# Eight weight pieces prepared beside the attention of two batches, and the first gate unit between its last steps

## Chip, cores and metric

The kernel runs on one core of a Trainium2 chip. Its time is the device time in microseconds, the median of several runs. Times inside it are from one profiled execution and count from the start of its span.

## What is computed

```
q, k, v: (4 batches, 12 heads, 448 tokens, 64); g_q, g_k: (64)
attn = softmax(rmsnorm(q, g_q) @ rmsnorm(k, g_k)^T / 8) @ v     # per batch and head
x = attn as (1792 tokens, 768)
y = (silu(x @ w_gate) * (x @ w_val)) @ w_out                    # 768 -> 1536 -> 768
h = y @ w2_in                                                   # 768 -> 2048
out = (h * cos(h)) @ w2_out                                     # 2048 -> 768, float32
```

Weights arrive as 64-bit floats. Each is turned into float32 by three VectorE instructions on its integer halves, scaled by a power of two and split into a high and a low 16-bit part; a product is then three matmuls.

## The kernel before

Heads go in pairs: pairs 0 to 5 are batch 0, 6 to 11 batch 1, and so on; a pair has seven steps of 128 rows (two heads of 448).

**Attention of batches 0 and 1.** One loop counts `n`. Step `n` of `c_step` makes the transposed scores of one row block (`c_st`, banks "c"), their exponential on ScalarE, and the product with V (`c_av`, banks "t" and "u"); twelve steps ahead `c_s` makes scores for the row maximum that VectorE takes from the three "s" banks. The row sums of a pair go through DRAM and back (`c_x`, `c_sum`, `c_inv`, `c_out`, `c_back`, `c_mul`, `c_lo`, over eleven steps) before its output `X` can be used; the last pair, 11, does it on the chip (`c_x`, `c_half`). The pair of batch 2 that comes next is prepared beside it.

**Weights.** A piece is three 128-row blocks of 256 columns. `w_load` brings it (768 KB, into one of three "raw" tiles), `w_conv` makes it float32 (VectorE L932 to L934) and sums its squares (ScalarE L952), `w_scale` makes the scale of a unit of two pieces from a small matmul (L959) and four small VectorE instructions, `w_split` makes the parts (ScalarE L964, VectorE L965), and the next `w_store` writes them to scratch (384 KB). Pieces 0 to 11 are gate and value units of columns 0 to 2 in turn (two gate pieces, two value pieces), 12 to 17 the output product of these columns, 18 to 35 the same again. The table `WSTEP` tells at which steps of the attention loop pieces are loaded, converted and split.

**Visits.** After that loop its pools are closed (the "c" and "u" banks become the four "mm" banks), and a visit runs the 18 matmuls of one piece on one batch (`mm_piece`, L1093 to L1095). Two pieces are visited for batch 0, then the same two for batch 1, 72 visits for pieces 0 to 35. Beside them run the 53 steps of the attention of batch 2, spread over the visits by `SCH`. At a piece's first visit `w_loads(j + LA)`, `w_conv(j + CA)`, `w_scale(j + CA - 1)` and `w_split(j + 2)` work ahead (`LA` 5, `CA` 4). `fin_gate` and `fin_val` take the banks out (ScalarE L1131, VectorE L1132, L1140).

**What sets the order.** A scheduler places instructions on each engine by its own timeline. What goes through `InOrder` stays in the order of the code while its engine is named in `in_order`: SP's queue and GpSimd during the attention loop. Through this helper all instructions show the helper's line (L156).

Of the kernel before, what the change touches and what calls it, by code (L numbers as in the profile page):

```python
# [164 lines left out]
def kernel(ctx: ExitStack, tc, q, k, v, g_q, g_k, w_gate, w_val, w_out, w2_in, w2_out, out):  # L165
# [3 lines left out]
    gps = InOrder(tc, nc.gpsimd, "POOL", in_order)  # L169
    B, H, S, D = q.shape  # L170
# [197 lines left out]
    def v_row(b):  # L368
        ps = bank(ps_s, "s")
        tc.keep_in_program_order(nc.tensor.matmul(ps[:1, :P], vmx.pop(b)[:, 2:3], ident, start=True, stop=True))  # L370
# [8 lines left out]
    def v_out(b):  # L379
        ps = bank(ps_s, "s")  # L380
        tc.keep_in_program_order(nc.tensor.matmul(ps[:, :2], full[:1], vmx.pop(b)[:, 2:4], start=True, stop=True))
# [87 lines left out]
    def s_mm(n):  # L469
# [6 lines left out]
        for i in range(2):  # L476
            for h in ((0, 1), (1, 0))[i]:
                hs = slice(HP * h, HP * h + HP)
                nc.tensor.matmul(  # L479
# [79 lines left out]
    def a_r(g):  # L559
        rd = Rs[g]  # L560
        if "rp" in cfg(g):
            ps = bank(ps_s, "s")
            nc.tensor.matmul(ps[:, :S], ones, rd.rearrange("p t q -> p (t q)"), start=True, stop=True)
# [11 lines left out]
    def a_av(g, part):  # L575
# [7 lines left out]
        for n in range(nn * part // 4, nn * (part + 1) // 4):  # L583
# [76 lines left out]
    def c_s(n):  # L660
# [26 lines left out]
    def c_st(n):  # L687
# [6 lines left out]
        for k, (wt, off, mv) in enumerate(((T, NS, T), (C, 0, Bq))):  # L694
            for h in ((0, 1) if h0 is None else (h0,)):
# [4 lines left out]
                nc.tensor.matmul(  # L700
# [4 lines left out]
    def c_av(g, j):  # L705
# [3 lines left out]
        for h in range(2):  # L709
# [3 lines left out]
            nc.tensor.matmul(pg["o"][h][:, :S], colv[g % 2][rows, j, h], e[rows], start=(j == 0), stop=(j == 3))  # L713
# [241 lines left out]
    def unit_scale(u):  # L955
        q = nrm_t.pop(u)
        ps = bank(ps_s, "s")
        for i, n in enumerate(q):
            nc.tensor.matmul(ps[:, :1], full, n[:, 0:1], start=(i == 0), stop=(i == len(q) - 1))  # L959
# [29 lines left out]

    def w_loads(upto):  # L990
# [7 lines left out]
    def w_conv(j):  # L998
        if j >= len(pieces) or not pieces[j]["fresh"] or pieces[j]["kind"] == "out2":
            return  # L1000
# [481 lines left out]
```

## Time and profile before

| | us |
|---|---|
| median of 3 runs | 1308.86 |
| the runs | 1307.93 to 1309.38 |
| the profiled execution, whole | 1306.7 |
| its span | 1304.9 |
| TensorE busy in the span | 1201.7 |
| VectorE busy | 830.6 |
| ScalarE busy | 646.2 |

The times in this document's rows are those of the profiled execution. It lies 2.2 us below the median. A matmul counts as busy to its modelled end, so that neighbours overlap; the pace is the distance of two starts.

### The profile page before, as it was taken

What the parts mean: (1) busy time and instruction counts of PE and PEld (TensorE: products, weight loads), DVE (VectorE), ACT (ScalarE), POOL (GpSimd) and SP (SyncE); (2) the same over time, 40 slices, a digit from 0 to 9 for tenths busy, and PEclk for the clock granted to TensorE, in tenths of its full rate; (3) what the DMA queues carried; (4) which work ended last, traced back from release to release, by engine and by line L of the source; (5) the groups of instructions that cost most, each with busy time, mean ns of one, the idle gap of its engine ahead of it and who ended that gap; (6) DMA issues with size and microseconds to landing.
All of it is one profiled execution on the core that took longest, in us unless ns stands there. A gap on an engine that the chain in (4) does not pass through costs nothing. (4 is left out here: it accounts for less than half of the span.)

```text
span 1304.9 us, 18162 instructions
## 1 busy us (share of the span) xinstructions
PE 1201.7 (92%) x6460; PEld 674.3 (52%) x6460; DVE 830.6 (64%) x1577; ACT 646.2 (50%) x1224; POOL 405.1 (31%) x309
## 2 busy tenths in 40 slices
PE   1898997888999979999999999999999998999998
PEld 0333333343774437744468546855555545666665
DVE  5876766989978896068844698487888885100000
ACT  3566673555555643356662454477776784100000
POOL 7755203344612254034552114413323222000000
PEclk9999998899999999999999999999999998999999
DMA  5544653866988778479768787630121237522121
GB/s 147 134 105 101 174 174 104 202 186 179 263 271 228 207 195 264 171 187 225 161 136 273 238 314 260 228 128 1 49 73 49 107 122 249 176 68 93 59 91 43
DMA packets 223532, 209.96 MB, mean 161 GB/s; under 512 B 147281, under 2 KB 178897, under 8 KB 223441
## 3 DMA queue, kind: packets, MB, share of 16 engines
q1 hardware_dynamic: 223440, 208.80, 55.4%
q8 instruction: 50, 0.82, 0.3%
q14 instruction: 42, 0.34, 0.1%
HBM read 136.87 MB, written 41.57 MB: 137 GB/s over the span
## 5 line engine op out<-in xcount | busy, mean ns | idle before, releaser
L1093 PE MATMUL mm<-xy,wp 128*128 128x448 f16 x840 | 299.9, 358 | 19.9 <-DVE ga L1132 7.0
L1094 PE MATMUL mm<-xy,wp 128*128 128x448 f16 x840 | 299.8, 357 | 0.8 <-POOL xy L156 0.8
L1095 PE MATMUL mm<-xy,wp 128*128 128x448 f16 x840 | 295.7, 356 | 2.2 <-DVE wp L965 2.2
L1106 PEld LDWEIGHTS <-g 128*128 128x128 f16 x1344 | 132.3, 98 | 92.8 <-issue 6.9
L1093 PEld LDWEIGHTS <-wp 128*128 128x128 f16 x960 | 96.5, 100 | 108.6 <-issue 18.7
L1094 PEld LDWEIGHTS <-wp 128*128 128x128 f16 x960 | 95.3, 99 | 95.8 <-issue 17.3
L1095 PEld LDWEIGHTS <-wp 128*128 128x128 f16 x960 | 94.6, 99 | 93.2 <-issue 5.7
L156 POOL TENSOR_TENSOR g<-tmp,g 128x448 f16<-128x448 f32 x64 | 71.0, 1123 | 175.5 <-ACT g L1252 175.5
L1093 PE MATMUL mm<-g,wp 128*128 128x448 f32 x288 | 106.9, 371 | 0.0
L1095 PE MATMUL mm<-g,wp 128*128 128x448 f32 x288 | 105.3, 366 | 0.0
L1094 PE MATMUL mm<-g,wp 128*128 128x448 f32 x288 | 104.7, 364 | 0.0
L1106 PE MATMUL mm<-wp,g 128*128 128x384 f16 x576 | 101.1, 330 | 3.8 <-DVE tmp L1248 3.8
L1106 PE MATMUL s<-wp,g 128*128 128x384 f16 x576 | 100.2, 328 | 0.0
L156 POOL TENSOR_TENSOR g<-ga,g 128x448 fp32r<-128x448 f32 x48 | 66.4, 1396 | 108.2 <-ACT g L1142 107.9
L498 ACT ACTIVATE pr<-s,sm,esc 128x448 f32<-128x448 f32 x84 | 60.2, 719 | 64.8 <-DVE sm L492 55.0
L156 POOL TENSOR_TENSOR wp<-w,wp 128x768 fp32r<-128x768 f32 x36 | 70.2, 1954 | 69.2 <-ACT wp L1033 44.0
L156 POOL TENSOR_TENSOR p<-pr,p 128x448 f16<-128x448 f32 x36 | 44.0, 1226 | 125.5 <-ACT p L522 83.4
L156 POOL TENSOR_TENSOR ri<-ss,half 128x14 f32<-128x14 f32 x24 | 63.9, 2662 | 57.1 <-DVE ss L347 32.2
L488 DVE TENSOR_REDUCE sm<-s 128x1 f32<-128x448 f32 x84 | 51.0, 615 | 45.0 <-PE s L479 44.9
L1264 ACT ACTIVATE tmp<-mm,osc 128x384 f32<-128x384 f32 x8 | 4.6, 580 | 148.6 <-PE mm L1106 147.8
L952 ACT ACTIVATE raw<-w 128x768 f32<-128x768 f32 x56 | 46.9, 838 | 54.6 <-DVE w L934 42.7
L932 DVE TENSOR_SCALAR w<-raw 128x768 int32<-128x768 int32 x68 | 49.7, 735 | 37.3 <-POOL wp L156 15.6
(179 smaller groups left out, 2258.5 us busy)
## 6 DMA issues: line engine op xcount, KB each, us to landing
raw<-in_moe_w_out_dram SPq DMA_DIRECT2D x28, 768.0 KB, 5.6
raw<-in_moe_w_in_dram SPq DMA_DIRECT2D x16, 768.0 KB, 5.8
raw<-in_moe_w_gate_dram SPq DMA_DIRECT2D x12, 768.0 KB, 5.5
raw<-in_moe_w_val_dram SPq DMA_DIRECT2D x12, 768.0 KB, 5.2
wp<-scr_gate SPq DMA_DIRECT2D x24, 384.0 KB, 4.6
w<-scr_out SPq DMA_DIRECT2D x24, 384.0 KB, 4.1
wp<-scr_val SPq DMA_DIRECT2D x24, 384.0 KB, 5.4
wp<-scr_out SPq DMA_DIRECT2D x24, 384.0 KB, 3.0
```

The lines of the kernel that those rows point to most:

```text
L156: r = f(*args, **kw)
L488: nc.vector.tensor_reduce(sm[:, 0, t:t + 1], slot[n][:, :S], axis=AX.X, op=ALU.max)
L498: nc.scalar.activation(e, slot.pop(n)[:, :S], AF.Exp, bias=sm[:, 1, t:t + 1], scale=esc, accum_out=sm[:, 2, t:t + 1],)
L932: nc.vector.tensor_scalar(wi, hi, 3, 0x3FFFFFF8, op0=ALU.logical_shift_left, op1=ALU.bitwise_and)
L952: nc.scalar.activation(sq_dst[0], w32, AF.Square, accum_out=n[:, 0:1])
L1093: nc.tensor.matmul(ps[f][:, :S], wh[:, s], x[:, 0], start=(first and i == 0), stop=False)
L1094: nc.tensor.matmul(ps[f][:, :S], wh[:, s], x[:, 1], start=False, stop=False)
L1095: nc.tensor.matmul(ps[f][:, :S], wl[:, s], x[:, 0], start=False, stop=(last and i == n - 1))
L1106: nc.tensor.matmul(ps[:, :CO], x[:, a, p0:p0 + P], rhs, start=st, stop=sp)
L1264: nc.scalar.activation(osb, ps[:, :CO], AF.Copy, scale=ci)
```

## The change

- `WSTEP` is built by a loop: pieces 0 to 7 are loaded, converted, scaled and split at steps 2 to 68 of the attention loop, a unit of two every 16 steps, and pieces 8 and 9 loaded and converted at steps 67 to 78.
- `mm_piece` can run some of a piece's three blocks. The 36 matmuls of the first gate unit on batch 0 run as six blocks at steps 75 to 80, into two "s" banks. Every matmul goes through `InOrder`, and from step 75 to the fourth visit TensorE keeps the order of the code.
- The first four pieces are visited for batch 0, then for batch 1. The first two visits have no matmuls left.
- For pieces below 12, conversion and split run two pieces further ahead (`ahead`), and loads up to 8; `once` keeps a piece from being prepared twice.
- The attention of batch 2 starts at visit 3, not 1.

Line numbers after the change are 7 to 18 higher; matmuls show the helper's line (L163).

```diff
@@ constants @@
+EARLY = 75
-WSTEP = {48: [("load", 2)], 56: [("conv", 0)], 60: [("conv", 1), ("load", 3)], 63: [("scale", 1)], 64: [("split", 0), ("conv", 2), ("load", 4)],
-         70: [("split", 1), ("conv", 3), ("load", 5)]}
+WL = 8
+WAHEAD = 4
+WSTEP = {}
+for _u in range(WAHEAD):
+    for _d, _w in ((-6, ("load", 0)), (-3, ("load", 1)), (0, ("conv", 0)), (4, ("conv", 1)), (7, ("scale", 1)), (8, ("split", 0)), (12, ("split", 1))):
+        WSTEP.setdefault(8 + 16 * _u + _d, []).append((_w[0], 2 * _u + _w[1]))
+for _n, _w in ((67, ("load", 8)), (70, ("load", 9)), (74, ("conv", 8)), (78, ("conv", 9))):
+    WSTEP.setdefault(_n, []).append(_w)
-SCH = ((1, 0), (0, 0), (1, 1))
+SCH = ((1, 0), (3, 0), (1, 1))
@@ w_loads @@
+            if 3 <= nload[0] < NJ and ("conv", nload[0] - 3) not in done:
+                return
@@ attention loop @@
+        if n == EARLY:
+            in_order.add("PE")
+        i = n - EARLY
+        if 0 <= i < KX:
+            if i == 0:
+                cur[0] = [bank(ps_s, "s") for _ in range(2)]
+            mm_piece(i // 3, cur[0], lambda kt: X[kt], (i % 3,))
         step(n, 0)
         w_store()
         w_step(n)
-    in_order.clear()
+    in_order.difference_update(("SP", "POOL"))
@@ visits @@
+    def ahead(j):
+        far = lambda near, t: near + 2 * (t < 2 * KX)
+        for f, near in ((w_conv, CA), (w_scale, CA - 1), (w_split, 2)):
+            for t in range(j, j + near + 3):
+                if t <= j + far(near, t):
+                    f(t)
-    for j0 in range(0, NJ, 2):
+    for j0, j1 in [(0, 4)] + [(j, j + 2) for j in range(4, NJ, 2)]:
         for b in range(2):
-            visits += [(j0, b), (j0 + 1, b)]
+            visits += [(j, b) for j in range(j0, j1)]
...
-                w_loads(j + LA)
+                w_loads(j + (WL if j + WL < 2 * KX else LA))
...
+            if i >= 2:
+                (first bank and mm_piece, as before)
             run_late(i)
             if new:
-                w_conv(j + CA)
-                w_scale(j + CA - 1)
-                w_split(j + 2)
+                ahead(j)
+            if i == 3:
+                in_order.clear()
```

**VectorE beside pairs 2 and 3.** Reductions of the scores are "sm", the integer halves "raw", the float32 piece "w32". Before:

```order
L670 TENSOR_REDUCE sm_836<-s_944 128x1
L677 TENSOR_SCALAR cw_357<-sm_836 128x7
L670 TENSOR_REDUCE sm_978<-s_979 128x1
L678 SCALAR_TENSOR_TENSOR cw_357<-sm_836,cw_357 128x7
L670 TENSOR_REDUCE sm_978<-s_989 128x1
L742 TENSOR_SCALAR sm_970<-sm_970,vsc_104 128x7
L398 TENSOR_TENSOR rqk_926<-rqk_926,ri_1096 128x448
L743 RECIPROCAL sm_970<-sm_970 128x7
L670 TENSOR_REDUCE sm_978<-s_1004 128x1
```

After the change, at the like place of the next pair but one:

```order
L678 TENSOR_REDUCE sm_860<-s_980 128x1
L940 TENSOR_SCALAR w32_1031<-raw_907 128x768
L685 TENSOR_SCALAR cw_357<-sm_860 128x7
L941 SCALAR_TENSOR_TENSOR w32_1031<-raw_907,w32_1031 128x768
L686 SCALAR_TENSOR_TENSOR cw_357<-sm_860,cw_357 128x7
L772 TENSOR_TENSOR tmp_1010<-co_814,cr_952 64x448
L942 SCALAR_TENSOR_TENSOR w32_1031<-raw_907,w32_1031 128x768
L772 TENSOR_TENSOR tmp_1010<-co_815,cr_952 64x448
```

The three conversion instructions of piece 2 now stand between those of the pair, one at a time.

**TensorE at the end of the attention.** "t" and "u" take the products with V, "c" the transposed scores, "s" the scores and now the gate unit ("wp" its weights, "xy" the output of a pair of batch 0). Before, the last steps and the first gate matmul:

```order
L700 MATMUL c_2103<-cB_1786,cC_415 128x448
L713 MATMUL u_2064<-pr_2076,cV_359 128x448
...
L713 MATMUL t_2063<-pr_2088,cV_359 128x448
L713 MATMUL u_2064<-pr_2104,cV_359 128x448
L713 MATMUL t_2063<-pr_2122,cV_359 128x448
L713 MATMUL u_2064<-pr_2122,cV_359 128x448
...
L1093 MATMUL mm_2188<-xy_831,wp_1816 128x448
```

After the change, from the last rows of scores that are turned ("id16") to the second block of the gate unit:

```order
L163 MATMUL s_2076<-id16_106,cw_419 64x128
...
L163 MATMUL s_2091<-xy_855,wp_866 128x448
...
L163 MATMUL s_2092<-xy_855,wp_866 128x448
...
L163 MATMUL c_2099<-T_1659 128x448
...
L163 MATMUL c_2099<-cB_1746,cC_353 128x448
...
L163 MATMUL s_2091<-xy_1009,wp_866 128x448
```

Six matmuls of the unit now stand ahead of each of six steps; the first "mm" matmul is of the value unit.

**VectorE at the joint.** L726 (now L734) is the reciprocal of the last pair, L419 (now L427) the subtraction of pair 12 that the load of pair 13 waits for, L764 (now L772) the last multiplication of a pair. Before:

```order
L764 TENSOR_TENSOR tmp_2071<-co_1940,cr_2039 64x448
L764 TENSOR_TENSOR tmp_2071<-co_1941,cr_2039 64x448
L742 TENSOR_SCALAR sm_2067<-sm_2067,vsc_104 128x7
L408 TENSOR_TENSOR rqk_1976<-rqk_1976,gk_94 128x448
L743 RECIPROCAL sm_2067<-sm_2067 128x7
L726 RECIPROCAL co_2138<-co_2138 128x448
L419 TENSOR_TENSOR h16_2053<-rqk_1976,h16_2053 128x7x64
L764 TENSOR_TENSOR tmp_2146<-co_2139,co_2138 128x448
```

After the change:

```order
L772 TENSOR_TENSOR tmp_2195<-co_2021,cr_2145 64x448
L772 TENSOR_TENSOR tmp_2195<-co_2022,cr_2145 64x448
...
L427 TENSOR_TENSOR h16_2165<-rqk_2056,h16_2165 128x7x64
...
L734 RECIPROCAL co_2268<-co_2268 128x448
...
L772 TENSOR_TENSOR tmp_2276<-co_2269,co_2268 128x448
L772 TENSOR_TENSOR tmp_2281<-co_2160,cr_2265 64x448
L772 TENSOR_TENSOR tmp_2281<-co_2161,cr_2265 64x448
```

The subtraction moved from behind the reciprocal to a place well ahead of it; the multiplication ahead of it is pair 9's in both.

## Rows read from the trace of the kernel before

**Rows 1.** stretches: PE, PEld, DVE, ACT, POOL busy (count), granted clock, DMA share, GB/s
```profile
57.00:139.00 82.00, 73.83 (x315) 28.42 (x314) 58.36 (x127) 54.75 (x100) 44.41 (x31) 0.98 0.49 119
...
206.00:333.50 127.50, 110.18 (x581) 52.31 (x580) 113.12 (x200) 64.76 (x129) 51.87 (x33) 0.94 0.67 174
333.50:390.00 56.50, 55.66 (x299) 45.32 (x298) 48.38 (x78) 30.81 (x76) 22.87 (x13) 1.00 0.94 272
390.00:505.00 115.00, 102.27 (x561) 51.25 (x562) 104.63 (x186) 61.35 (x122) 42.69 (x29) 0.97 0.81 228
...
214.30:333.50 119.20, 101.93 (x546) 48.38 (x544) 108.54 (x195) 62.46 (x125) 51.87 (x33) 0.94 0.68 177
```

**Rows 2.** waits of TensorE, 206 to 333.5 us: total, times, longest
```profile
PE mm L1093 <- ACT wp L964: 5.7, 4, 3.6
```

**Rows 3.** timeline of TensorE at the joints: start, us, instruction, wait ahead
```profile
192.51 1.02 PE L713 MATMUL t<-pr,cV 128*128 128x448 f32 x2 [1.29 <-ACT pr L703]
...
199.54 0.54 PE L713 MATMUL u<-pr,cV 64*128 64x448 f32 x1
206.05 0.53 PE L1093 MATMUL mm<-xy,wp 128*128 128x448 f16 x1 [5.97 <-ACT co L725]
...
214.05 0.35 PE L1095 MATMUL mm<-xy,wp 128*128 128x448 f16 x1
214.24 0.35 PE L1093 MATMUL mm<-xy,wp 128*128 128x448 f16 x1
...
333.49 0.47 PE L1093 MATMUL mm<-g,wp 128*128 128x448 f32 x1
```

**Rows 4.** groups of VectorE and ScalarE, 0 to 206 us: total, mean ns
```profile
L934 DVE SCALAR_TENSOR_TENSOR w<-raw,w 128x768 int32<-128x768 int32 x5 | 4.7, 947 | 0.0
...
L933 DVE SCALAR_TENSOR_TENSOR w<-raw,w 128x768 int32<-128x768 int32 x5 | 4.7, 938 | 0.0
...
L932 DVE TENSOR_SCALAR w<-raw 128x768 int32<-128x768 int32 x5 | 2.7, 547 | 0.0
...
L965 DVE SCALAR_TENSOR_TENSOR wp<-w,wsc,wp 128x768 f16<-128x768 f32 x2 | 2.1, 1036 | 0.4 <-ACT wp L964 0.4
...
L952 ACT ACTIVATE raw<-w 128x768 f32<-128x768 f32 x5 | 4.2, 840 | 0.0
L964 ACT ACTIVATE wp<-w,wsc 128x768 f16<-128x768 f32 x2 | 1.7, 920 | 0.0
```

**Rows 5.** timeline of TensorE, first product with V of pairs 3 and 7
```profile
85.38 1.02 PE L713 MATMUL t<-pr,cV 128*128 128x448 f32 x2 [1.36 <-ACT pr L703]
...
140.62 1.02 PE L713 MATMUL t<-pr,cV 128*128 128x448 f32 x2
```

**Rows 6.** two-operand VectorE lines: mean in 57 to 139; min, median, max
```profile
L398 DVE TENSOR_TENSOR rqk<-rqk,ri 128x448 f32<-128x448 f32 x7 | 5.6, 805 | 0.2 <-POOL ri L156 0.2
...
L398 DVE TENSOR_TENSOR rqk<-rqk,ri x12: 604/618/1369, 13.9 to 134.1; 128x448 f32<-128x448 f32 x12
...
L934 DVE SCALAR_TENSOR_TENSOR w<-raw,w x11: 941/950/2369, 240.5 to 332.2; 128x768 int32<-128x768 int32 x11
```

**Rows 7.** the burst: busy time of ten us, TensorE's wait behind it
```profile
136.00:146.00 10.00, 10.00 (x40) 3.63 (x39) 9.61 (x16) 7.58 (x14) 0.00 (x0) 1.00 0.83 258
...
154.35 1.86 PE L713 MATMUL t<-pr,cV 128*128 128x448 f32 x2 [1.93 <-ACT pr L703]
```

**Rows 8.** timeline of ScalarE, first and last copy of the last pair
```profile
202.95 0.54 ACT L722 ACTIVATE co<-t 64x448 f32<-64x448 f32 x1 [1.77 <-DVE tmp L764]
...
205.37 0.63 ACT L725 ACTIVATE co<-u,vs 64x448 f32<-64x448 f32 x1
```

**Rows 9.** SP's queue at the load of pair 13, TensorE at pair 10
```profile
SPq L156 <- DVE h L419: 23.6, 4, 11.5
...
208.87 0.35 SPq L156 DMA_DIRECT2D rqk<-in_k_dram  x1
...
222.71 0.54 PE L1093 MATMUL mm<-xy,wp 128*128 128x448 f16 x2 [0.69 <-ACT xy L765]
```

More of the change, by code (lines that the diff above doesn't have):

```diff
@@ L169 @@
     gps = InOrder(tc, nc.gpsimd, "POOL", in_order)
+    pe = InOrder(tc, nc.tensor, "PE", in_order)
     B, H, S, D = q.shape
@@ L380, in v_out @@
         ps = bank(ps_s, "s")
-        tc.keep_in_program_order(nc.tensor.matmul(ps[:, :2], full[:1], vmx.pop(b)[:, 2:4], start=True, stop=True))
+        tc.keep_in_program_order(pe.matmul(ps[:, :2], full[:1], vmx.pop(b)[:, 2:4], start=True, stop=True))
         nc.vector.tensor_copy(vsc[:, 2 * b:2 * b + 2], ps[:, :2])
@@ L562, in a_r @@
             ps = bank(ps_s, "s")
-            nc.tensor.matmul(ps[:, :S], ones, rd.rearrange("p t q -> p (t q)"), start=True, stop=True)
+            pe.matmul(ps[:, :S], ones, rd.rearrange("p t q -> p (t q)"), start=True, stop=True)
             if "rv" in cfg(g):
@@ L712, in c_av @@
             e = col[g, 2 * j + h] if j < 3 else col[g, NS - 1]
-            nc.tensor.matmul(pg["o"][h][:, :S], colv[g % 2][rows, j, h], e[rows], start=(j == 0), stop=(j == 3))
+            pe.matmul(pg["o"][h][:, :S], colv[g % 2][rows, j, h], e[rows], start=(j == 0), stop=(j == 3))
     def c_x(g):
@@ L958, in unit_scale @@
         for i, n in enumerate(q):
-            nc.tensor.matmul(ps[:, :1], full, n[:, 0:1], start=(i == 0), stop=(i == len(q) - 1))
+            pe.matmul(ps[:, :1], full, n[:, 0:1], start=(i == 0), stop=(i == len(q) - 1))
         pow2_scale(ps[:, :1], winv[:, u:u + 1], wsc[:, u:u + 1])
@@ L988, with once @@
     nload = [0]
+    done = set()
+    def once(what, j):
+        new = (what, j) not in done
+        done.add((what, j))
+        return new
     def w_loads(upto):
@@ L998, in w_conv @@
     def w_conv(j):
-        if j >= len(pieces) or not pieces[j]["fresh"] or pieces[j]["kind"] == "out2":
+        if j >= len(pieces) or not pieces[j]["fresh"] or pieces[j]["kind"] == "out2" or not once("conv", j):
             return
@@ L1006, in w_scale @@
     def w_scale(j):
-        if j < len(pieces) and pieces[j]["fresh"] and pieces[j]["last"] and pieces[j]["kind"] in ("gate", "val", "h"):
+        if j < len(pieces) and once("scale", j) and pieces[j]["fresh"] and pieces[j]["last"] and pieces[j]["kind"] in ("gate", "val", "h"):
             unit_scale(unit_of(pieces[j]))
     def w_split(j):
-        if j >= len(pieces) or not (pieces[j]["fresh"] or pieces[j]["kind"] == "out1"):
+        if j >= len(pieces) or not (pieces[j]["fresh"] or pieces[j]["kind"] == "out1") or not once("split", j):
             return
@@ L1082, in pre_step, with mm_piece @@
         return done
-    def mm_piece(j, ps, rhs):
+    def mm_piece(j, ps, rhs, steps=None):
         pc = pieces[j]
@@ L1088, in mm_piece @@
         wh, wl = wp_t[j]
-        for i in range(n):
+        for i in range(n) if steps is None else steps:
             x = rhs(pc["k0"] + i)
@@ L1092, in mm_piece @@
                 s = slice(i * 256 + f * P, i * 256 + (f + 1) * P)
-                nc.tensor.matmul(ps[f][:, :S], wh[:, s], x[:, 0], start=(first and i == 0), stop=False)
-                nc.tensor.matmul(ps[f][:, :S], wh[:, s], x[:, 1], start=False, stop=False)
-                nc.tensor.matmul(ps[f][:, :S], wl[:, s], x[:, 0], start=False, stop=(last and i == n - 1))
+                pe.matmul(ps[f][:, :S], wh[:, s], x[:, 0], start=(first and i == 0), stop=False)
+                pe.matmul(ps[f][:, :S], wh[:, s], x[:, 1], start=False, stop=False)
+                pe.matmul(ps[f][:, :S], wl[:, s], x[:, 0], start=False, stop=(last and i == n - 1))
     def mm_out(j, i, ps):
@@ L1105, in mm_out @@
                 st, sp = first and kk == 0 and a == 0 and rhs is wh, last and kk == n - 1 and a == 1
-                nc.tensor.matmul(ps[:, :CO], x[:, a, p0:p0 + P], rhs, start=st, stop=sp)
+                pe.matmul(ps[:, :CO], x[:, a, p0:p0 + P], rhs, start=st, stop=sp)
     def out2_w(j, kk):
@@ L1167, in y_scale @@
         ps = bank(ps_s, "s")
-        nc.tensor.matmul(ps[:, :1], full, n[:, 0:1], start=True, stop=True)
+        pe.matmul(ps[:, :1], full, n[:, 0:1], start=True, stop=True)
         pow2_scale(ps[:, :1], ysc[:, B + b:B + b + 1], ysc[:, b:b + 1])
```

20 lines of the change are left out of this document (10 added, 10 removed).

## The prediction

> **What bounds the kernel now.** I read the stages first: busy time and granted clock in stretches [rows 1]. Up to 206 us the attention of batches 0 and 1 runs; to 333.5 come 24 visits of gate and value pieces (a visit is the 18 matmuls of one weight piece on one batch); to 390 twelve visits of the first output product; to 505 the same 24 visits again with the second half of the columns. In the first set TensorE was busy 110.2 of 127.5 us at a mean clock of 0.94, VectorE 113.1. The second set lasted 115.0 us with VectorE at 104.6. In both, VectorE carries conversions and splits beside the attention of batch 2, and it is the fuller engine.
>
> Next, who TensorE waits for in the first set: 6.0 us for the last copies of the attention stage [rows 3], then 5.7 for the high halves of weights [rows 2]. The times of the joints are read off the timeline [rows 3]: attention ends at 199.54 + 0.54 = 200.1; the first gate matmul starts at 206.05, after a wait of 5.97; its unit has 36 matmuls, and the 37th starts at 214.24, by then 0.187 us after the one before it, the pace of the upper clock level. The first output matmul starts at 333.49.
>
> What must remain of the 119.2 us from 214.3 on? TensorE was busy for 101.9 of them, and a mean clock of 0.94 means that 12% of the stretch stood at the lower level, where half the time is lost: 0.06 x 119.2 = 7.2. So 94.8 us of work at the upper level [rows 1], 17.2 idle, 7.2 to the clock.
>
> **The change part by part.**
>
> *Conversions and splits moved ahead.* Before 206 us VectorE converts 5 pieces and splits 2 [rows 4]; the order puts 11 and 8 ahead of the first gate step. Six more of each: 6 x (0.547 + 0.938 + 0.947) = 14.6 us and 6 x 1.036 = 6.2 [rows 4], with an estimated 1.8 for the scales of three units (small instructions of some 0.15 us): 22.6 us. ScalarE gets 6 x (0.84 + 0.92) = 10.6 us [rows 4]; it was busy 54.8 of 82 us there [rows 1], so there is room.
>
> They fall on steps 8 to 52. A pair's first product with V is step 2 of its seven; pair 3's (step 23) stands at 85.4 and pair 7's (step 51) at 140.6 [rows 5], so a step takes 2.0 us and the six extra pieces land between about 57 and 143. VectorE was busy for 58.4 of the 82 us from 57 to 139 [rows 1]. 58.4 + 22.6 = 81.0: full, before any stall. Stalls there are: GpSimd is busy 44.4 of those 82 us [rows 1], and the two-operand product at L398 took 0.805 us in the mean against 0.604 at best over the stage [rows 6]. At 0.2 us for each of 18 two-operand instructions that is 3.6 us more: 84.6 of the 86 us.
>
> TensorE is what sets the pace there (73.8 of 82 us busy), so what counts is how often it then waits. The nearest row is the one burst that the kernel already has: about 140 to 152 us three conversions beside the largest-value search filled VectorE to 9.6 of 10 us [rows 7]. TensorE then waited 1.93 us for ScalarE, and the product behind the wait took 1.86 us against 1.02 elsewhere [rows 5, 7], a sign of the lower clock level: some 3.5 us for 10.4 us of extra VectorE work (three conversions of 2.43 and the search). Spread out, each of six pairs gets 3.0 + 0.6, a third of that burst: 6 x 1.2 = 7 us, less about 2 because this burst loses its three conversions. I take **5 us**. Ends: -3.5 (the burst's cost goes, nothing comes), and 6 x 3.5 - 3.5 = 17.5 (every pair pays the burst's price).
>
> SP's queue gets 6 loads and 6 stores of 768 and 384 KB, 7.1 MB, put between the transposes and the round trip of the row sums, and a store waits at the head of the queue for its split. About 82 GB/s over 86 us on top of 119 at a DMA share of 0.49; the chip moved 272 at 0.94 later [rows 1]. Behind those waits stand the round trips, eight steps ahead of need, so I cost them at nothing; if that cover is gone, the price is in the 17.5.
>
> *The first gate unit between the steps of the last two pairs.* TensorE runs there without gaps but for 1.29 us [rows 3], so 36 x 0.187 = 6.7 us are added, less the 1.3 that they cover, plus about 0.7 until ScalarE has emptied the two "s" banks that they need: the attention ends at 206.2 without the 5 us above, 211.2 with it. Then the four copies of the last pair must end before "mm" banks exist: before, ScalarE stood behind a VectorE multiplication until 202.95, and the last of the copies began at 205.37 [rows 8]. Here what hangs on that multiplication (pair 9's) stands ahead of the last four exponentials on ScalarE, so it is done by then (were its round trip late, it would now hold them, and TensorE; that is in the 17.5); four copies of 0.54 to 0.63 make 2.3 us, with the hand-over 2.6: 213.8. That is the point that the kernel before reached at 214.3. The gate unit by itself therefore gains what the 5 us cost, and little more. The two "s" banks stay taken until the gate's activation reads them; one is left for the scores of batch 2, which now start at visit 3.
>
> What could be late next is batch 1: its gate unit needs pair 10. Before, the load of pair 13 stood at the head of SP's queue until 208.87, released by VectorE's L419, and behind it pair 10's round trip; TensorE got pair 10 at 222.71 [rows 9]. The order now puts the subtraction L427 (the old L419) that this load waits for ahead of the last pair's reciprocal, not behind it; and TensorE has 36 value and 24 gate matmuls, some 12 us, to do first. Covered.
>
> *The 22 visits that remain.* They are the 94.8 us. From the order, up to the last value step of this set VectorE now has 8 conversions and 4 splits in place of 11 and 10 (it also takes up later pieces sooner): 3 x 2.43 + 6 x 1.04 = 13.5 us less, of 108.5. The kernel before took 119.2 us with 108.5 of VectorE work, the second set 115.0 with 104.6 [rows 1]: both 10.5 us longer than VectorE's work. So 108.5 - 13.5 = 95.0 for VectorE and 94.8 for TensorE: about **105 us**, a loss of 10. Ends: 4 (TensorE 96% busy) and 16 (the second set's loss: 12.7 idle, 3.5 clock).
>
> *After 333.5.* The loads and the output visits stand as before; TensorE was at 55.7 of 56.5 us there. The last 4071 matmuls and 794 VectorE instructions stand in the same order as before. A shift should be kept.
>
> *Sum.* 213.8 + 104.8 = 318.6 against 333.5: 14.9 us less. The profiled execution was 1306.7, so 1291.8; the median of the runs shown is 1308.86, 2.2 above it, so 1294.0. I say **1293**.
>
> **The rivals.**
>
> *Nothing waits in the attention stage, and the visits run as TensorE alone would* (0 and 4 in place of 5 and 10): 11 us more gain, 1282. For: order spreads the conversions one instruction between two reductions. Against: VectorE's 81 of 82 us.
>
> *The visits stay VectorE's*, because the conversions that come sooner fill what was freed (loss 16), or the stage pays more (11): 6 us less gain for each, 12 for both: 1299 to 1305. For: all that is freed is 13.5 us, and VectorE and TensorE are then level.
>
> *Slower: VectorE becomes the bound of the attention stage.* GpSimd and VectorE hold each other up: in the visits L934 took up to 2.369 us against 0.941 at best [rows 6]. If every L933, L934 and L965 of the six pieces met such a stall (1.43 us), VectorE would need 58.4 + 22.6 + 25.7 = 106.7 us in 86. The stage then grows by 21 us, and by more where VectorE also waits for transfers; from 5 + 14.9 = 20 us on, the change loses. 1310 to 1315. Against: GpSimd is idle for half the stretch, and L398's mean shows 0.2, not 1.4. The Trainium skill, "SBUF — State Buffer", section "Who interferes with whom", has a rule for this: a VectorE instruction with two inputs in SBUF and a GpSimd instruction that reads SBUF exclude each other, and the later one blocks entirely. By that rule, 18 instructions met at a share of 0.54 by 1.43 us of GpSimd work, half of it left, wait 18 x 0.54 x 0.72 = 7.0 us, not 3.6; the estimate would then be some 3 us slower, 1296. L398 at 0.805 agrees in kind, with a smaller number.
>
> **How the numbers follow.** Forecast 0.50 (1287 to 1298), larger gain 0.20 (1280 to 1287), smaller gain 0.20 (1298 to 1307), slower 0.10. 0.2% is 2.6 us, about what a measurement of this kernel can tell from no change; of the smaller gain 0.04 lies within it, of the slower case 0.02. Faster 0.86, the same 0.06, slower 0.08. For 8 in 10 the range leaves out the lower end of the larger gain (0.07), the last us of the smaller (0.03) and the slower case: 1282 to 1305.
>
> **What would show it.** The first "mm" matmul near 214 us after a wait of 2 to 3 us in place of 6; in 57 to 143, VectorE above 9 tenths and TensorE's waits for L678 and L711 (the old L670 and L703) up by some 5 us; the first output matmul near 319; from there on the same lengths. Wrong if the attention stage grew by over 10 us, if the visits from the first "mm" to the first output matmul still take over 111 us, or if the second set (115 us) changes by more than 3.

## The result, and the profile after

The changed kernel takes 1298.46 us (median of 4 runs; the kernel before, beside it, 1308.95): a ratio of 0.9919, 95% interval 0.9899 to 0.9938, 10.5 us less. The forecast was 1293, the range 1282 to 1305. The profiled execution has a span of 1297.1 us against 1304.9, so 7.8 of the gain show in it. The total came out near the forecast by luck: the attention stage came out 12.7 us later than summed and the visits 6.7 us shorter, and these errors went opposite ways.

The stages, first of the kernel before (length, then busy time of TensorE, weight loads, VectorE, ScalarE, GpSimd, granted clock, DMA share, GB/s): from the first product with V to the end of the attention of batches 0 and 1, from the first "mm" matmul to the first output matmul, the twelve output visits, the second set of gate and value visits. In the kernel before the second of these stretches still holds the first gate unit; from the 37th matmul on it was 119.2 us [rows 1].

```profile
43.30:200.07 156.77, 143.36 (x609) 55.97 (x607) 112.22 (x237) 104.12 (x190) 61.32 (x45) 0.98 0.55 143
206.05:333.49 127.44, 110.17 (x580) 52.30 (x579) 113.06 (x200) 64.72 (x129) 51.86 (x33) 0.94 0.67 174
333.49:386.10 52.61, 51.77 (x277) 43.07 (x275) 45.10 (x72) 27.86 (x67) 22.88 (x13) 1.00 0.97 283
386.10:499.68 113.58, 100.85 (x558) 48.49 (x557) 102.61 (x187) 62.38 (x125) 40.46 (x27) 0.97 0.80 224
```

The same view of the changed kernel, with the stretch from 57 to 139 us as its second row:

```profile
43.40:223.85 180.45, 153.79 (x657) 63.08 (x655) 140.25 (x287) 116.24 (x213) 67.23 (x47) 0.93 0.63 170
57.00:139.00 82.00, 69.07 (x281) 27.74 (x282) 67.61 (x139) 55.24 (x102) 39.49 (x26) 0.88 0.54 137
226.34:324.47 98.13, 92.40 (x517) 44.30 (x516) 84.33 (x141) 48.92 (x97) 46.38 (x31) 0.98 0.61 155
324.47:385.44 60.97, 56.21 (x288) 44.26 (x287) 48.55 (x85) 35.01 (x82) 22.25 (x15) 0.97 0.78 220
385.44:489.20 103.76, 99.17 (x558) 48.84 (x557) 93.11 (x173) 58.84 (x120) 38.47 (x26) 0.98 0.83 224
```

The attention stage is 23.7 us longer, the visits 29.3 shorter (21.1 from the same point on), the output visits 8.4 longer, the second set 9.8 shorter. From 57 to 139 us VectorE was busy 67.6 of 82 us, not the 81 of the sum, and TensorE 69.1 at a mean clock of 0.88 where it had 73.8 at 0.98 [rows 1]; fewer steps fit into the same time.

The joints in TensorE's timeline of the changed kernel (start, us, instruction, wait ahead), which answer to [rows 3]:

```profile
132.62 1.01 PE L163 MATMUL s<-id,cw 128*64 128x128 f16 x7 [6.72 <-DVE sm L678]
...
192.43 1.02 PE L163 MATMUL t<-pr,cV 128*128 128x448 f32 x2
...
200.43 0.95 PE L163 MATMUL s<-id,cw 128*64 128x128 f16 x7 [3.98 <-DVE cw L686]
201.32 2.33 PE L163 MATMUL s<-xy,wp 128*128 128x448 f16 x6
...
223.31 0.54 PE L163 MATMUL t<-pr,cV 64*128 64x448 f32 x1
...
226.34 5.25 PE L163 MATMUL mm<-xy,wp 128*128 128x448 f16 x18 [2.49 <-ACT co L733]
...
324.47 3.94 PE L163 MATMUL mm<-g,wp 128*128 128x448 f32 x18
```

The attention ends at 223.31 + 0.54 = 223.9 (before 200.1). The wait for the last copies is 2.49 in place of 5.97. The two largest waits inside the attention, 6.72 and 3.98 us, have no counterpart in the kernel before, where the largest after 57 us was 1.93 [rows 7]. The row at 192.43 is pair 10's first product with V; the gate unit's first block follows within this pair. What VectorE did ahead of the first of the two waits:

```profile
119.61 0.19 DVE L686 SCALAR_TENSOR_TENSOR cw<-sm,cw 128x7 f16<-128x7 f32 x1
125.96 0.56 DVE L940 TENSOR_SCALAR w<-raw 128x768 int32<-128x768 int32 x1 [6.17 <-DMA raw<-in_moe_w_gate_dram]
...
131.96 1.14 DVE L678 TENSOR_REDUCE sm<-s 128x1 f32<-128x448 f32 x2
```

At 119.8 us VectorE's next instruction was the conversion L940 of a piece that had not landed; it stood for 6.17 us. The row maxima L678, on which TensorE's score banks wait, came only at 131.96, behind this and behind 6.0 us of other work that stood between. SP's queue in the same stretch:

```profile
110.36 1.55 SPq L163 DMA_TRANSPOSE T<-h  x1
117.79 0.35 SPq L163 DMA_DIRECT2D rc<-sm  x1
118.24 0.37 SPq L163 DMA_DIRECT2D scr_val<-wp  x1
118.67 0.42 SPq L163 DMA_DIRECT2D raw<-in_moe_w_gate_dram  x1
```

SP had stood from 111.9 to 117.79 before the write of the row sums (rc), waiting for VectorE's reciprocal L751. Behind that write stood a store of a split (scr) and the load, so the piece was issued 7.3 us ahead of its use.

### The profile page after: what moved, and what is told of

The parts are those of the page before. It is cut to its first block, busy times and chain, and to the rows that moved or that the text cites. A ratio compares the mean times of both kernels' runs of the same rounds, so it can differ in the third digit from the quotient of the medians.

```text
span 1297.1 us, 18102 instructions
## 1 busy us (share of the span) xinstructions
PE 1198.0 (92%) x6460; PEld 676.1 (52%) x6460; DVE 831.3 (64%) x1577; ACT 645.6 (50%) x1224; POOL 406.8 (31%) x309
## 5 line engine op out<-in xcount | busy, mean ns | idle before, releaser
L163 PE MATMUL mm<-xy,wp 128*128 128x448 f16 x2484 | 491.0, 354 | 5.8 <-DVE ga L1149 3.2
L163 PEld LDWEIGHTS <-wp 128*128 128x128 f16 x2880 | 277.9, 99 | 278.5 <-issue 34.5
L163 PE MATMUL mm<-g,wp 128*128 128x448 f32 x864 | 185.4, 372 | 1.9 <-DVE ga L1157 1.9
L163 PEld LDWEIGHTS <-g 128*128 128x128 f16 x1344 | 132.0, 98 | 91.9 <-issue 5.7
L163 PEld LDWEIGHTS mm<-g,wp 128*128 128x128 f32 x864 | 162.6, 191 | 20.5 <-issue 4.4
L163 POOL TENSOR_TENSOR g<-tmp,g 128x448 f16<-128x448 f32 x64 | 71.2, 1124 | 174.8 <-ACT g L1269 174.8
L163 POOL TENSOR_TENSOR g<-ga,g 128x448 fp32r<-128x448 f32 x48 | 64.8, 1362 | 146.6 <-ACT g L1159 146.5
L163 PE MATMUL mm<-wp,g 128*128 128x384 f16 x576 | 100.8, 330 | 3.6 <-DVE tmp L1265 3.6
L163 PE MATMUL s<-wp,g 128*128 128x384 f16 x576 | 99.3, 326 | 0.0
L163 PE MATMUL s<-T 128*64 128x448 f16 x336 | 63.2, 396 | 36.1 <-DVE T L665 22.6
L163 POOL TENSOR_TENSOR wp<-w,wp 128x768 fp32r<-128x768 f32 x36 | 72.7, 2024 | 59.7 <-ACT wp L1050 39.2
L163 PEld LDWEIGHTS <-T 128*64 128x64 f16 (+1 forms) x432 | 28.4, 109 | 106.5 <-issue 78.5
L942 DVE SCALAR_TENSOR_TENSOR w<-raw,w 128x768 int32<-128x768 int32 x68 | 77.3, 1137 | 0.6
L940 DVE TENSOR_SCALAR w<-raw 128x768 int32<-128x768 int32 x68 | 46.0, 679 | 49.0 <-POOL wp L163 10.6
L163 POOL TENSOR_TENSOR ri<-ss,half 128x14 f32<-128x14 f32 x24 | 63.9, 2663 | 42.3 <-DVE ss L355 33.5
L941 DVE SCALAR_TENSOR_TENSOR w<-raw,w 128x768 int32<-128x768 int32 x68 | 72.5, 1068 | 0.6
L163 POOL TENSOR_TENSOR p<-pr,p 128x448 f16<-128x448 f32 x36 | 41.1, 1147 | 88.0 <-ACT p L530 70.9
```

The lines of the kernel that those rows point to most:

```text
L163: r = f(*args, **kw)
L940: nc.vector.tensor_scalar(wi, hi, 3, 0x3FFFFFF8, op0=ALU.logical_shift_left, op1=ALU.bitwise_and)
L941: nc.vector.scalar_tensor_tensor(wi, hi, -0x40000000, wi, op0=ALU.bitwise_and, op1=ALU.bitwise_or)
L942: nc.vector.scalar_tensor_tensor(wi, lo, 29, wi, op0=ALU.logical_shift_right, op1=ALU.bitwise_or)
```

## Experiments

Each is the changed kernel with the edit shown; lines of an edit are cut to the part that changes. The attention's end is the start of the last "t" matmul plus its 0.54 us, "pair 10" the start of its first product with V. These times are of one profiled execution each; the ratios are medians, to the kernel before on the same chip.

| | ratio | 95% interval | pair 10 | attention ends | first "mm" | first output matmul |
|---|---|---|---|---|---|---|
| kernel before | 1 | | 180.8 | 200.1 | 206.1 | 333.5 |
| changed kernel | 0.9919 | 0.9899–0.9938 | 192.4 | 223.9 | 226.3 | 324.5 |
| loads earlier | 0.9959 | 0.9943–0.9975 | 195.3 | 231.0 | 233.5 | 332.8 |
| pieces only | 0.9958 | 0.9942–0.9975 | 195.5 | 215.0 | 218.9 | 328.5 |
| gate unit only | 0.9997 | 0.9981–1.0012 | 182.6 | 212.8 | 228.8 | 332.6 |
| loads later | 0.9923 | 0.9902–0.9944 | 194.8 | 224.0 | 226.9 | 325.3 |
| short conversions | 0.9949 | 0.9927–0.9972 | 194.7 | 228.5 | 232.9 | 331.4 |
| no loads | 0.9922 | 0.9897–0.9948 | 196.2 | 226.8 | 229.3 | 329.0 |
| three units | 0.9907 | 0.9878–0.9935 | 190.9 | 221.8 | 224.3 | 324.5 |
| two units | 0.9999 | 0.9983–1.0015 | 192.9 | 223.3 | 227.6 | 333.1 |
| products later | 0.9921 | 0.9897–0.9944 | 194.7 | 223.9 | 226.4 | 325.7 |
| both later | 0.9921 | 0.9897–0.9946 | 195.0 | 223.5 | 226.0 | 325.6 |
| order only | 0.9907 | 0.9882–0.9932 | 190.3 | 223.5 | 226.0 | 324.4 |
| units later | 0.9884 | 0.9853–0.9915 | 183.4 | 213.0 | 215.5 | 321.9 |

**The two parts, each alone.** Pieces only:

```
-EARLY = 75
+EARLY = 10 ** 6
-            if i >= 2:
+            if True:
```

> The changed kernel with the first gate unit back behind the attention (the pieces are still prepared beside it). By the prediction's sum the unit's move saves the wait for the last copies (6.0 against 2.6 us) and the 1.3 us that it covers, less some 0.7: the attention then ends at 216 to 217 in place of 223.9, the first mm matmul comes at about 222 and the time is 1301 to 1303. Rival: the unit between the steps costs TensorE as much as it saves, since the 4.0 us wait at 200 us and the lower clock of its first block (2.33 against 1.30 us) come with it: 1296 to 1299.

Gate unit only:

```
-WL = 8
-WAHEAD = 4
-WSTEP = {}
...
+WL = 5
+WSTEP = {48: [("load", 2)], 56: [("conv", 0)], 60: [("conv", 1), ("load", 3)], 63: [("scale", 1)], 64: [("split", 0), ("conv", 2), ("load", 4)],
+         70: [("split", 1), ("conv", 3), ("load", 5)]}
-SCH = ((1, 0), (3, 0), (1, 1))
+SCH = ((1, 0), (0, 0), (1, 1))
-        far = lambda near, t: near + 2 * (t < 2 * KX)
+        far = lambda near, t: near
```

> The changed kernel with the piece preparation of the kernel before (five conversions and two splits beside the attention), the first gate unit still between the last pair's steps. Theory: the gain comes from the visits, which took 98.1 us from the first mm matmul against 119.2 from the same point before, and that needs the pieces prepared ahead; without them the attention ends near 207, the first mm matmul comes near 210, the visits take 115 to 120 us, and the time is 1304 to 1308. Rival: the gate unit's move and the other order of the first visits bring the gain: 1296 to 1300.

The pieces alone give 0.9958 and cost the attention 215.0 - 200.1 = 14.9 us; the gate unit then adds some 5 us of gain by the ratios (0.9958 to 0.9919, measured on different chips, the intervals just apart). Alone it gives nothing (0.9997), and its attention ended at 212.8, not near the 207 expected. The kernel before, the gate unit only and the pieces only, from pair 10 on:

```profile
180.76 1.02 PE L713 MATMUL t<-pr,cV 128*128 128x448 f32 x2
...
187.69 0.58 PE L682 MATMUL s<-id,cw 128*64 128x128 f16 x7 [0.36 <-DVE cw L678]
```

```profile
182.64 1.02 PE L159 MATMUL t<-pr,cV 128*128 128x448 f32 x2
...
190.23 0.80 PE L159 MATMUL s<-id,cw 128*64 128x128 f16 x7 [3.04 <-DVE cw L682]
...
220.98 1.01 PE L159 MATMUL s<-nm,full 128*128 128x1 f32 x4 [7.41 <-ACT pr L502]
...
228.82 0.93 PE L159 MATMUL mm<-xy,wp 128*128 128x448 f16 x2 [0.65 <-ACT wp L968]
```

```profile
195.47 1.02 PE L163 MATMUL t<-pr,cV 128*128 128x448 f32 x2
...
218.91 12.06 PE L163 MATMUL mm<-xy,wp 128*128 128x448 f16 x54 [3.93 <-ACT co L733]
```

This splits the cost of the two parts. Up to pair 10, ahead of the gate unit's first step, the kernels with the pieces are late (changed kernel 192.4 - 180.8 = 11.7 us, pieces only 14.7), the gate unit alone hardly (1.9). From pair 10 to the end the kernel before took 19.3 us and the pieces only 19.5, but the gate unit only 30.1 and the changed kernel 31.4. So the gate unit costs the attention 10.8 to 12.1 us. A part is the wait for "cw" (3.04 and 3.98 us): with TensorE in the order of the code these seven matmuls stand ahead of the unit's first block, where in the kernel before they came after the pair's third product and waited 0.36. That is not all of it: five kernels without a large wait there (loads later, two units, products later, both later, units later) still take 28.4 to 30.4 us.

After the attention of the gate unit only there is no prepared piece left to work on: the first value matmul comes at 228.82, 16 us later. Part of that may be this kernel's own: batch 2's attention starts at the first visit again, and the matmul for the scale of the value pieces waits 7.41 us for ScalarE's L502, which reads batch 2's scores out of a score bank, while the gate unit holds two of the three. In the pieces only, the unit's 36 matmuls run behind the attention, and the 37th comes at about 227.4 (an estimate: 54 matmuls from 218.91, the last 18 at 0.187 us), 1.1 us after the changed kernel's first value matmul. So at the joint the unit's move gains about 1 us; the rest of its gain comes in the visits (first output matmul 4.0 us earlier), and why was not tried.

**Late loads?** The loads of pieces 2 to 9 six steps earlier, and in another kernel three steps later:

```
-    for _d, _w in ((-6, ("load", 0)), (-3, ("load", 1)), (0, ("conv", 0)),
+    for _d, _w in (((-12, -6)[_u == 0], ("load", 0)), ((-9, -3)[_u == 0], ("load", 1)), (0, ("conv", 0)),
-for _n, _w in ((67, ("load", 8)), (70, ("load", 9)),
+for _n, _w in ((60, ("load", 8)), (63, ("load", 9)),
```

> The changed kernel with the loads of weight pieces 2 to 9 issued six steps earlier (seven for pieces 8 and 9); conversions, splits and the gate unit stay where they are. Theory 1, late loads: the attention stage grew because VectorE, which works in order, stands 12.4 us at L940 for pieces that are issued only some 7 us ahead, 6.17 us of it at one piece (TensorE then waits 6.7 us for the row maxima L678 queued behind) and about 3 us ahead of the 3.98 us wait for cw at 200 us. Then the first mm matmul comes at 215 to 218 us in place of 226.3 and the time is 1288 to 1292. Theory 2, VectorE is full: the six extra conversions and splits fill it, whoever it waits for; the waits move to the next row maximum, the first mm matmul stays within 2 us of 226 and the time within 1296 to 1300. Theory 3, VectorE held up by GpSimd: as theory 2, 1296 to 1300.

```
-    for _d, _w in ((-6, ("load", 0)), (-3, ("load", 1)), (0, ("conv", 0)),
+    for _d, _w in (((-3, -6)[_u == 0], ("load", 0)), ((0, -3)[_u == 0], ("load", 1)), (0, ("conv", 0)),
-for _n, _w in ((67, ("load", 8)), (70, ("load", 9)),
+for _n, _w in ((70, ("load", 8)), (73, ("load", 9)),
```

> The changed kernel with the loads of pieces 2 to 9 issued three steps (some 6 us) later, nothing else. Late loads (theory 1): VectorE stands up to 6 us more at each of the eight pieces, and TensorE behind it; with at least half of them reaching TensorE the attention stage grows by 15 to 40 us and the time is 1313 to 1338. VectorE full or held up by GpSimd (theories 2 and 3): the loads are hidden, 1296 to 1301.

Theory 1 fell both ways: earlier loads made the kernel slower by the ratio, later ones changed nothing. (With the loads earlier theories 2 and 3 missed too: first "mm" at 233.5, not within 2 us of 226.) The 6.7 us wait was gone in both, but others came. With the loads earlier, in TensorE's timeline:

```profile
163.92 1.01 PE L163 MATMUL s<-id,cw 128*64 128x128 f16 x7 [5.26 <-DVE sm L678]
```

With the loads later TensorE waited 3.46 us for L678 at 177.7.

**How much work, or how many bytes?** Conversions cut to one of three instructions, and the loads left out:

```
+        if short:
+            return w32
-        w32_t[j] = conv64(raw_t.pop(j))
+        w32_t[j] = conv64(raw_t.pop(j), 2 <= j < 8)
```

> The changed kernel with the conversions of pieces 2 to 7 cut from three VectorE instructions to the first (L941 and L942 left out: 12 instructions of 0.95 us, 11.4 us less VectorE work beside the attention; its weights are therefore wrong). Loads, splits, stores and the gate unit stay. Theory F, the amount of VectorE work fills the engine, and whatever comes late beside it reaches TensorE: the attention ends 7 to 12 us earlier (212 to 217 us in place of 223.9) and the time is 1287 to 1292. Theory L, what costs is the loads and stores in SP's queue and the landing of the pieces: the attention ends at 221 to 226 and the time is 1296 to 1300.

```
+            if 2 <= j < 8:
+                raw_t[j] = raw_t[1, 0]
+                return
...
```

(The rest of the edit keeps piece 1's raw tile in place for this.)

> The changed kernel without the loads of pieces 2 to 7 (4.6 MB beside the attention left out; their conversions read the raw tile of piece 1 again, so its weights are wrong; one mask differs), with the same number of conversions, splits and stores. Theory L: VectorE no longer waits 9 us for pieces 2 to 7, the attention ends at 212 to 217 us and the time is 1287 to 1292. Theory F: VectorE is as full as before, the attention ends at 220 to 226 and the time is 1295 to 1300.

Neither theory held: with 11.4 us of VectorE instructions left out (its busy time fell from 140.3 to 132.9) the attention ended at 228.5, without the loads at 226.8. From the first product with V to the end, with the short conversions:

```profile
42.80:228.46 185.66, 154.98 (x657) 62.50 (x655) 132.87 (x282) 116.07 (x213) 69.15 (x48) 0.95 0.61 167
```

The same without the loads:

```profile
43.40:226.77 183.37, 159.25 (x657) 63.33 (x655) 141.40 (x289) 117.10 (x213) 69.10 (x47) 0.92 0.54 143
```

TensorE stood idle for 185.7 - 155.0 = 30.7 and 183.4 - 159.3 = 24.1 us, against 26.7 in the changed kernel and 13.4 before. So neither half of the added VectorE work nor the loads alone set the end.

**How many units?**

```
-WAHEAD = 4
+WAHEAD = 3
-for _n, _w in ((67, ("load", 8)), (70, ("load", 9)), (74, ("conv", 8)), (78, ("conv", 9))):
+for _n, _w in ((67, ("load", 6)), (70, ("load", 7)), (74, ("conv", 6)), (78, ("conv", 7))):
```

> The changed kernel with three units (six pieces and two conversions) prepared beside the attention in place of four (eight and two). If each unit costs the attention the same (from the gate-only kernel to the changed one it ends 11.1 us later for some three units more, and the visits up to the first output product get 19.2 us shorter): attention end at 220, first output matmul at 327, time 1300 to 1302. Rival: the last unit is the one that overfills VectorE; then the attention ends at 215 to 217 and the time is 1293 to 1297.

```
-WAHEAD = 4
+WAHEAD = 2
-for _n, _w in ((67, ("load", 8)), (70, ("load", 9)), (74, ("conv", 8)), (78, ("conv", 9))):
+for _n, _w in ((67, ("load", 4)), (70, ("load", 5)), (74, ("conv", 4)), (78, ("conv", 5))):
```

> The changed kernel with two units (four pieces and two conversions) prepared beside the attention. If each unit costs and gains the same: attention end at 216.5 us, first output matmul at 330, time 1302 to 1305. Rival, the cost is not in proportion and the last two units overfill VectorE: attention end at 210 to 213, time 1293 to 1298.

The cost is not per unit. With three units the attention ends at 221.8 (220 expected, 215 to 217 by the rival) and the first output matmul comes at 324.5 as with four, not at 327. With half the units the attention ends where it did with all, at 223.3, and since the visits gain little the kernel is as slow as before. Up to 200 us this kernel converts 7 pieces and splits 4, the kernel before 5 and 2, and yet it reaches pair 10 12.1 us later. Its timeline near the first large wait (VectorE, then TensorE):

```profile
125.84 1.27 DVE L772 TENSOR_TENSOR tmp<-co,cr 64x448 f32<-64x448 f32 x2 [4.37 <-DMA cr<-rc]
...
130.87 1.01 PE L163 MATMUL s<-id,cw 128*64 128x128 f16 x7 [4.58 <-DVE sm L678]
```

No load stands there, and yet VectorE waits 4.37 us, now for the row sums' round trip (cr) at L772, with the row maxima (at 130.21) behind it.

**Taking the waiting product out of the way.** Row maxima and the products L772 kept in program order on VectorE ("order only"):

```
+    dve = InOrder(tc, nc.vector, "DVE", in_order)
-        nc.vector.tensor_reduce(pg["m"][:, 0, t:t + 1], ps[:, :S], axis=AX.X, op=ALU.max)
+        dve.tensor_reduce(pg["m"][:, 0, t:t + 1], ps[:, :S], axis=AX.X, op=ALU.max)
-            nc.vector.tensor_tensor(xs[rows], src[rows], r[rows], op=ALU.mult)
+            dve.tensor_tensor(xs[rows], src[rows], r[rows], op=ALU.mult)
...
```

(`in_order` names VectorE during the attention loop.)

> The changed kernel with only the order kept of the row maxima (L678) and the products with the row sums (L772) on VectorE, both at the steps where they were. It tells the order from the later step. Theory R: the order already puts some row maxima ahead of the product that waits; the attention ends at 216 to 221 us and the time is 1291 to 1296. Theory C: 221 to 227 us and 1296 to 1301.

To this, for "products later":

```
-CXL = 11
+CXL = 14
-(c_mul, 8), (c_lo, CXL)
+(c_mul, 11), (c_lo, CXL)
```

> The changed kernel with VectorE's row maxima (L678) and its products with the returned row sums (L772) kept in program order beside the attention, and these products three steps later, so that a late round trip of the row sums no longer stands ahead of the next pair's first row maxima. Work, loads, stores and the gate unit are unchanged. Theory R: TensorE waits because VectorE stands, in order, for round trips (3 to 4 us at 122 us in the kernel with two units) and landings with row maxima queued behind; taken out of the way, the attention ends at 212 to 219 us in place of 223.9 and the time is 1287 to 1294. Theory C, whichever wait is taken away, another takes its place, since each of the single changes so far left the end between 222 and 231: the attention ends at 220 to 227 and the time is 1295 to 1301.

And to that, for "both later", with the three conversion instructions in program order too:

```
-(0, ("conv", 0)), (4, ("conv", 1)), (7, ("scale", 1)), (8, ("split", 0)), (12, ("split", 1))
+(4, ("conv", 0)), (8, ("conv", 1)), (11, ("scale", 1)), (12, ("split", 0)), (16, ("split", 1))
-(74, ("conv", 8)), (78, ("conv", 9))
+(78, ("conv", 8)), (82, ("conv", 9))
```

> As the kernel before it (row maxima and products with the row sums in order, the products three steps later), and the conversions, scales and splits of the pieces four steps later behind their loads, in order too, so that a load has some 20 us in place of 12 to be landed. Theory R with late landings as the second part: VectorE's waits for pieces (12.4 us in the changed kernel) are gone as well, the attention ends at 209 to 215 us, the time is 1284 to 1290. Theory C: 220 to 227 us and 1295 to 1301.

Theory R fell, and theory C held, in all three, though the waits that theory R named went: VectorE waited 7.1 us for cr and 12.4 for pieces in the changed kernel's attention, and with both later 2.8 for cr and none for pieces. From the first product with V to the end, with the products later:

```profile
45.40:223.92 178.52, 157.92 (x657) 63.61 (x655) 137.01 (x283) 115.33 (x209) 62.47 (x45) 0.94 0.61 168
```

The same with both later:

```profile
45.90:223.48 177.58, 157.33 (x657) 63.02 (x655) 136.47 (x279) 112.58 (x205) 61.67 (x45) 0.94 0.59 158
```

Idle time came down from 26.7 to 20.6 and 20.3 us, but the same 657 matmuls were busy for 157.9 and 157.3 us in place of 153.8. The clock does not explain that: the mean granted clock was 0.94 in both, against 0.93 in the changed kernel. Why the busy time rose stays open. The end did not move.

**The place.** Three units again, later in the attention (and 14 steps apart instead of 16), nothing else:

```
-        WSTEP.setdefault(8 + 16 * _u + _d, [])
+        WSTEP.setdefault(30 + 14 * _u + _d, [])
...
```

> The kernel with three units (first output matmul 324.5 us, attention end 221.8, pair 6 at 137.4 against 127.7 in the kernel before) with its units at steps 30, 44 and 58 in place of 8, 24 and 40; the same pieces, instructions, transfers and gate unit. Theory P, the place: up to step 56 VectorE also prepares the queries and keys of the pairs to come and has no room for whole round trips, from about 140 us on it has; the delay of some 9 us that every version with early units collects by pair 6 goes. Pair 6 comes at 127 to 131 us, the attention ends at 211 to 217, and the time is 1288 to 1294. Theory C, the delay moves to wherever the units stand: the attention ends at 220 to 226 us and the time is 1296 to 1301.

Theory P held for the attention; its reason, that VectorE has room for whole round trips there, was not tried. With the early units, from the first product with V to the end, and TensorE's timeline at pair 6:

```profile
42.00:221.80 179.80, 151.89 (x653) 61.53 (x651) 135.00 (x275) 112.81 (x208) 66.22 (x47) 0.94 0.58 158
```

```profile
132.84 1.01 PE L163 MATMUL s<-id,cw 128*64 128x128 f16 x7 [8.34 <-DVE sm L678]
...
137.36 1.86 PE L163 MATMUL t<-pr,cV 128*128 128x448 f32 x2
```

With the later units, the same stretch:

```profile
42.10:213.02 170.92, 153.44 (x653) 60.62 (x651) 133.96 (x272) 112.54 (x205) 64.90 (x47) 0.96 0.58 160
```

And TensorE's timeline at pairs 6 and 10 and the end:

```profile
126.06 1.02 PE L163 MATMUL t<-pr,cV 128*128 128x448 f32 x2
...
183.41 1.02 PE L163 MATMUL t<-pr,cV 128*128 128x448 f32 x2
...
212.48 0.54 PE L163 MATMUL t<-pr,cV 64*128 64x448 f32 x1
```

Pair 6 comes at 126.1 (127.7 in the kernel before, 137.4 with early units, 132.4 to 137.7 in the other kernels that have them), pair 10 only 2.7 us later than before, and the attention ends at 213.0, 8.8 us earlier, for the same pieces. VectorE's busy time in it is nearly the same, 134.0 against 135.0. The first output matmul is only 2.6 us earlier, because the visits then take 106.4 us in place of 100.2. The kernel has the lowest ratio of all, 0.9884, but its interval meets those of the changed kernel and of three early units: that the whole kernel is faster for it is not shown, only that this stage is shorter.

What differs in the queues: SP's waits for the reciprocal of the row sums, in the changed kernel (us in total, times, longest) over its attention:

```profile
SPq L163 <- DVE sm L751: 20.4, 7, 6.6
```

And with the later units:

```profile
SPq L163 <- DVE sm L751: 8.0, 6, 3.5
```

In the kernel before they were 10.6 us. That would fit an early backlog on VectorE which delays row sums, and through SP's queue every transfer behind them. But it is not shown as the cause, and two kernels speak against it as the whole of it: with the order only these waits are 4.0 us and with both later 4.8, and the end stays at 223.5.

## Why the prediction was right in sum and wrong in its terms

- **Conversions and splits in the attention: 5 us taken, 11.7 measured** at pair 10 (192.4 - 180.8; 14.7 with the pieces only), inside the ends of -3.5 and 17.5. The step that failed is "full, before any stall, but spread out, each pair gets a third of the burst". VectorE was not full (67.6 of 82 us), and what came were not six small delays: 9.4 of the 11.7 us had come by pair 6, 6.7 of them in one wait with the lower clock around it. The cost hangs on the place more than on the amount: the later units reach pair 10 2.7 us late, two early units 12.1. What in the early place makes the delay was not found. VectorE standing in order for round trips and landings is the reading nearest at hand, but with both later these waits were nearly gone and pair 10 came at 195.0.
- **The gate unit: 6.1 us taken for the attention, 12.1 measured** from pair 10 on (31.4 against 19.3), 10.8 in the kernel with the unit alone. The sum had the 36 matmuls at 6.7 us and a cover of 1.3; it did not have that TensorE, kept in the order of the code, would stand 3.98 us for "cw" ahead of the unit's first block, nor that this block would run at the lower clock level (2.33 us against 1.30 for the blocks behind it). The rest is open. The wait for the last copies came as forecast, 2.49 us for 2.6. That the unit is worth some 5 us beside the pieces agrees with the sum in size alone: at the joint it gains about 1 us.
- **The joint.** The first "mm" came at 226.3, not 213.8: 6.7 us from the pieces and 6.0 from the unit, less 0.1 at the copies.
- **SP's queue at nothing: not shown wrong.** VectorE did wait 12.4 us for pieces to land, which the sum did not have, but for cr it waited less than before (7.1 us against 13.7), and leaving the loads out brought the end no earlier. Leaving out the stores was not tried.
- **The 22 visits: 104.8 us forecast, 98.1 measured.** TensorE had less work there than the 94.8 us: 517 matmuls in place of 546 [rows 1], while 12 more stand in the attention stage beside the unit's 36 and 11 more in the output visits. Worked out as the prediction did, 92.4 busy less 0.02 x 98.1 = 2.0 for the clock leaves 90.4, and a loss of 7.7 where 10 was taken. VectorE had 84.3 us of work there, not 95.0; 3.5 us more of it stands in the output visits (48.6 against 45.1), and the attention took 28.0 more, not 22.6. The order of the queue to the same instruction does not tell in which stage work is done when stages change length.
- **"A shift should be kept": wrong by its own test.** (So is the attention stage, which grew by more than 10 us; but the sum itself had 11.1 there.) The second set changed by 9.8 us, the output visits by 8.4 the other way. In the output visits TensorE ran 288 matmuls in place of 277 and waited for batch 2's attention, which starts later (view of waits, 324.4 to 385.5 us):

```profile
PE s L163 <- ACT pr L506: 2.3, 1, 2.3
PE s L163 <- DVE vm L373: 1.5, 1, 1.5
```

  From the end of the second set on, the gain is 499.7 - 489.2 = 10.5, and 2.7 of it is lost over the remaining 805 us. Why the second set is shorter was not tried. VectorE had 9.5 us less to do in it (two or three conversions fewer) and 8.7 us more behind it, so work moved out of it; its waits fell with that (before, 5.7 us for ga and 5.4 for the squares of raw; after, 2.2 for ga).
- **The rivals.** "Larger gain" was right for the time of the visits and wrong for the attention; "smaller gain" the reverse, and about half of the one was made up by the other: 12.5 us lost, 6.7 gained, 1.2 lost after that, which is the 7.1 (rounded) between the 14.9 forecast and the 7.8 in the span. That the sum still came near is luck, not a sign that its terms were right. The slower case, every moved instruction stalled by GpSimd for 1.43 us, is refuted by durations. VectorE's lines from 57 to 200 us of the changed kernel (count, total, mean ns):

```profile
L942 DVE SCALAR_TENSOR_TENSOR w<-raw,w 128x768 int32<-128x768 int32 x9 | 9.4, 1045 | 0.1
L973 DVE SCALAR_TENSOR_TENSOR wp<-w,wsc,wp 128x768 f16<-128x768 f32 x8 | 8.6, 1080 | 0.3 <-ACT wp L972 0.3
L941 DVE SCALAR_TENSOR_TENSOR w<-raw,w 128x768 int32<-128x768 int32 x8 | 7.6, 948 | 0.0
...
L406 DVE TENSOR_TENSOR rqk<-rqk,ri 128x448 f32<-128x448 f32 x7 | 4.3, 612 | 0.7 <-POOL ri L163 0.7
```

  Against their shortest of 943, 1001 and 936 ns, the moved lines lost 0.9 + 0.6 + 0.1 = 1.6 us; L406 (the old L398) took 612 ns, less than before [rows 6]. The exclusion of the Trainium skill, "SBUF — State Buffer", section "Who interferes with whom", would have made 7.0 us of it by the prediction's estimate; here the trace does not agree with that size.

**What stays open.** Nine kernels with early units and the gate unit, each with one or two suspects changed, reach pair 10 between 190.3 and 196.2 us and end the attention between 221 and 231. Waits moved from one instruction to another, and no queue that was looked at explains it. Only the place of the units moved pair 10 back.

## To carry to other kernels

Idle time of an engine is not yet room: the sum of busy times fitted here, and the stage grew all the same. When work is moved into a stage that is bound elsewhere, try two places before judging the amount; here the place was worth 8.8 us of stage time, and two, three or four early units cost much the same. When two parts of a change fall into one stage, read a time between them and run each part alone before putting the cost down to one of them. And when stages change length, sum the price at the end of the next stages, not at the first joint.

## Hardware behaviour that was not expected

A small write landed later where large transfers had been issued just ahead of it. SP's queue of the changed kernel with a store of 384 KB and a load of 768 KB ahead of the row sums' 3.5 KB write:

```profile
81.96 0.36 SPq L163 DMA_DIRECT2D scr_gate<-wp  x1
82.37 0.42 SPq L163 DMA_DIRECT2D raw<-in_moe_w_val_dram  x1
82.89 0.50 SPq L163 DMA_DIRECT2D rc<-sm  x1
87.59 1.12 SPq L163 DMA_DIRECT2D cr<-rc  x2
```

The read back (cr), which needs that write, could be issued 4.70 us after it; the write itself landed after 4.7 us. At a second such place (166.48) it was 3.82. In the kernel before, with nothing large ahead:

```profile
118.43 0.35 SPq L156 DMA_DIRECT2D rc<-sm  x1
119.99 1.12 SPq L156 DMA_DIRECT2D cr<-rc  x2
```

There it was 1.56 us, and the write landed after 1.5. This was read from these places, not tried by itself; another write of the kernel before, with no weights just ahead (75.06), also took 3.07.
